# One more unit of a gated recurrence read "by squares", with four small moves around it, in a fused recurrence and SwiGLU kernel

## The chip, the cores and the metric

The kernel runs on one core of a Trainium2 chip. The metric is the device time of one execution in microseconds (us). The kernel before takes 600.96 us, the median of three runs between 600.88 and 601.17 us.

## The reference, cut to what matters

There are 4 batches, 8 heads, 768 time steps and a head dimension of 48. The recurrence's output is laid out as 3072 tokens of 384 values and goes through a feed-forward block.

```python
f = 1.0 / (1.0 + np.exp(-f_logit))
for t in range(S):
    state = f[:, :, t, :, None] * state + np.einsum('bhd,bhe->bhde', k[:, :, t], v[:, :, t])
    y[:, :, t] = np.einsum('bhd,bhde->bhe', q[:, :, t], state)
x = y.transpose(0, 2, 1, 3).reshape(B * S, H * D)          # 3072 x 384
g = x @ w_gate                                             # 384 x 1536
out = (g / (1 + np.exp(-g)) * (x @ w_val)) @ w_out         # 1536 x 384
```

The weights arrive as 64-bit floats and the four recurrence inputs as 32-bit floats.

## The kernel before, in words

**Tiling.** A *unit* u is one batch b of one chunk c of 128 time steps; there are 6 chunks of 4 batches, so u = 4c + b runs from 0 to 23. Within a unit the recurrence is done in closed form: running products of f scale k and q, TensorE forms the 128 x 128 scores (`sc`), VectorE masks them (`A`), and TensorE adds the part from the state (`y`) and forms the chunk's contribution to the next state (`dS`). A chunk's outputs of all four batches form `xT[c]`, 384 features by 512 tokens, on which the feed-forward block of that chunk runs while the next chunk's units are computed. This case concerns chunk 0's end and chunk 1 (units 4 to 7), which lie in the first 140 us. Chunk 0's feed-forward (`mlp_plain`) consists of 12 *gate* products and 12 *val* products (L808; I number them 0 to 11, in the order gate 0, val 0, gate 1, val 1, gates 2 and 3, vals 2 and 3, and so on in pairs), and then 12 *down* steps (L831) of four matrix products each, one per batch. The outputs of gate, val and down steps take turns in four PSUM banks (tag `m`): each may start when the bank's older tile has been read, a gate by ScalarE's Silu (L818), a val by VectorE's multiply (L822).

**Two ways to turn f, k and q.** They arrive with time on the partitions and are needed with features on the partitions. Units 0 to 5 use TensorE transposes (L595, four per input). From unit 6 on, `by_squares(u)` holds: four DMAs per input (L447) lay the data out so that VectorE's 32 x 32 stream transposes finish the job (f in L609, k in L620, q in L658). Units 6 and 7 also send their decayed k through DRAM instead of transposing it on TensorE (L676): VectorE turns it in squares (L642), four DMAs write it (L645) and one reads it back as `kt` (L683), all on GpSimd's queue.

**Weights.** A piece of 64-bit weights is fetched by SyncE's queue (L472, four buffers `w64`), read by two ScalarE passes (`sizes`: L489 into `up`, L491 into `top`, two buffers each) and put together by four VectorE instructions (`join`: L500, L502, L504, L506). An `up` buffer is free again after its L506.

**Order.** Each engine's order up to about 45 us is written by hand, and from there it follows the program: `attention_steps(1)` cuts each unit of chunk 1 into four steps, which `take_turns` interleaves with the gate, val and down pieces. The loads of v, and of f, k, q for units before 6, are issued by SyncE's queue (L455); v of units 6 and 7 and the loads by squares of those units are issued by GpSimd's. `load(B + 1)` loads unit 5. The least product of each unit is kept in `least`; for units by squares ScalarE copies it (L652).

Of the kernel before, what the change touches and what calls it, by code (L numbers as in the profile page):

```python
# [290 lines left out]
def short_path(ctx, tc, ident, least, judge, q, k, v, f_logit, moe_w_gate, moe_w_val, moe_w_out, out):  # L291
# [9 lines left out]
    nc = tc.nc  # L301
    B, H, S, D = q.shape
# [13 lines left out]
    SQUARES = 2  # L316
# [47 lines left out]
    def pairs(t, off=0):  # L364
        return t[:, off:off + HP * N1].rearrange("p (a t) -> p a t", t=N1)
# [33 lines left out]
    rooms = {nm: t.rearrange("p n h w -> p (n h w)")[:, 0:Q + HP * RUN] for nm, t in both_raw.items()}  # L399

    def by_squares(u):
        return u >= SQUARES * B - 2

    def make_rooms(pool):
        for nm in "fkq":
# [3 lines left out]
    def v_of(u):  # L409
        return vs[u % (NV if units[u][1] < SQUARES else NV // 2)]  # L410
# [20 lines left out]
    def load(u, what="fkqv"):  # L431
        b, c = units[u]
        rows = slice(c * C, (c + 1) * C)
        inputs = dict(f=f_logit, k=k, q=q, v=v)
        for nm in "fqkv" if c >= SQUARES else "fvkq" if by_squares(u) else "fkqv":
            src = inputs[nm]
            if nm not in what:
                continue
            if nm == "v":
                dst = v_of(u)  # L440
            elif not by_squares(u):
                dst = raw[nm][u % NRAW]
            else:
                since = len(traced)
                for n in range(4):
                    at = Q * (1 - n % 2)
                    (nc.sync if c >= SQUARES else nc.gpsimd).dma_start(  # L447
                        out=rooms[nm][Q * n:Q * (n + 1), at:at + HP * RUN].rearrange("t (a e) -> t a e", a=HP),
                        in_=src[b, n // 2::2, rows, :].rearrange("a (t i) d -> t a (i d)", i=NI))
                if c < SQUARES:  # L450
                    by_pool.extend(ins for ins in traced[since:] if ins.engine == mybir.EngineType.Pool)
                    keep_order(by_pool[-5:])
                continue
            queue = nc.gpsimd if c < SQUARES and by_squares(u) else nc.sync
            queue.dma_start(out=dst[:, :, 0:D], in_=src[b, :, rows, :].rearrange("h t d -> t h d"))  # L455

    def weight_piece(dst, src, parts):
# [60 lines left out]
    fetches, sizes, joins = [], [], []  # L518
# [29 lines left out]
    def bank(name):  # L548
        return banks[-1].tile([128, 512], FP32, tag="a", name=name)
# [10 lines left out]
    def attention(u):  # L560
        b, c = units[u]
# [30 lines left out]
        def transposed(name, src):  # L592
            p = bank(name)
            for a in range(HP):
                nc.tensor.transpose(p[:, a * C:(a + 1) * C],  # L595
                                    src[:, 2 * a:2 * a + 2, :].rearrange("t r d -> t (r d)"), ident)
            return p.rearrange("p (a t) -> p a t", t=C)
# [6 lines left out]
        else:  # L604
            p = transposed("fTp", fr)
# [22 lines left out]
        whole = pairs(tail)[:, :, 1:2]  # L628
        nc.vector.reciprocal(pairs(start)[:, :, 0:1], whole)
        yield  # L630
        if not in_squares:
            kp = transposed("kTp", kr)
            qp = transposed("qTp", qr)
            if by_squares(u + 1):
                load(u + 1)
# [13 lines left out]

        if in_squares:  # L650

            nc.scalar.copy(least[:, u, :], whole.rearrange("p a t -> p (a t)"))  # L652
            whole = least[:, u, :].unsqueeze(2)
        nc.vector.tensor_tensor_scan(gate[:, 0:n], gate[:, 0:n], start, 1.0, op0=ALU.mult, op1=ALU.add)
        yield
# [17 lines left out]
        if c < NCH - 1 and not turned:  # L673
            p = bank("kt")
# [21 lines left out]
        if c and b < B - 1:  # L696
# [20 lines left out]
            for h in range(H):  # L717
                a, par = h // 2, h % 2
# [31 lines left out]
        if c < NCH - 1:  # L750
            p = bank("dS")
# [4 lines left out]
        if c >= SQUARES and u + 2 < len(units):  # L756
            load(u + 2, "v")
# [7 lines left out]
    def load_after(u, what):  # L765

        if u + 1 < len(units) and u + 1 != SQUARES * B:
            load(u + 1, what)

    def attention_steps(c):  # L770

        runs = [attention(c * B + b) for b in range(B)]
        order = sorted((2 * b + s, b, n) for b in range(B)
                       for s, n in enumerate((1, 8, 3, 3) if by_squares(c * B + b) else (3, 6, 3, 3)))
        return [lambda b=b, n=n: [next(runs[b]) for _ in range(n)] for _, b, n in order]
# [9 lines left out]
    def keep_order(mine):  # L785
        for a, b in zip(mine, mine[1:]):
            tc.add_manual_dep(b, a.name, mybir.DependencyInfo(mybir.DependencyClass.NoSync,
                                                              mybir.DependencyReason.DATA), reason="order")
# [89 lines left out]
    whole = NJ * TRIPLE + 7 * DOWN  # L878
# [328 lines left out]
    def weights():  # L1207
        if fetches:
            fetches.pop(0)()
        if sizes:  # L1210
            sizes.pop(0)()
        if joins:
            joins.pop(0)()
# [5 lines left out]
    mark = traced[-1]  # L1219
    keep_warm(5)  # L1220
    first = [attention(b) for b in range(B)]
    done = [0] * B

    def run(b, *steps):
        for s in steps:
            assert done[b] == s
            done[b] += 1
            for _ in range((3, 1, 5, 3, 3)[s]):
                next(first[b])
# [27 lines left out]
    sizes.pop(0)()  # L1257
    run(B - 1, 3)
    first_join(("add",))
    sizes.pop(0)()  # L1260
    joins.pop(0)()
    run(B - 1, 4)

    hidden, last = mlp_plain(0)
    steps = attention_steps(1)
# [7 lines left out]
    joins.pop(0)()  # L1273
    hidden[1]()
    weights()
    load(B + 1)
    hidden[2]()
    steps.pop(0)()
    in_order(mark, (mybir.EngineType.PE, mybir.EngineType.DVE, mybir.EngineType.Activation, mybir.EngineType.SP))
# [29 lines left out]
    for c in range(2, NCH):  # L1309
        for b in range(B):  # L1310
            run = attention(c * B + b)
            waiting += [((c - 2) * whole + t, lambda run=run: next(run)) for t in times(c)[b]]
# [33 lines left out]
def kernel(  # L1346
# [22 lines left out]
    def judge(bank):  # L1369
# [13 lines left out]
        yield  # L1383

    short_path(tc, ident, least, judge, *args)
    with tc.If(redo[0] > 0, label="redo"):
        general_path(tc, *args)
# [32 lines left out]
```

## Time and profile before

| what | value |
|---|---|
| median of three runs | 600.96 us |
| the profiled execution | 601.18 us |
| its span on the core | 599.4 us |
| granted TensorE clock | 0.999 |
| busy share of the span: TensorE, VectorE, ScalarE, GpSimd | 98%, 80%, 49%, 15% |
| HBM read and written | 46.27 and 7.34 MB |

The profiled execution has 1.78 us outside its span and lies 0.22 us above the median. A row of the timeline gives a start, a duration, the engine, the line of the kernel, the operation, out<-in, and in brackets the idle time just before it with what ended it. Rows of the same form that follow each other are merged, with their count; the duration is then that of the whole row. Successive instructions overlap by some 0.07 us, so that the distance between two starts is what an instruction costs its engine.

### The profile page before, as it was taken

The numbers are of one execution on the slowest core, as the hardware profiler recorded it, in microseconds if no ns is written. First come the engines' busy times: TensorE is split into PE (matmuls) and PEld (weight loads), VectorE is DVE, ScalarE is ACT, GpSimd is POOL, SyncE is SP. The second block draws the span as 40 slices with busy tenths as digits, with TensorE's granted clock in tenths as the row PEclk, the third lists the DMA queues.
The fourth block names the chain that finished last, engine by engine and source line by source line (L and its number), as shares of the span: only waits on it lengthen the run. The fifth ranks groups of instructions, "written<-read, shape, count | busy, mean of one in ns | idle before, by whom it ended". The sixth has DMA issues, their size and how long they took to land.

```text
span 599.4 us, 10862 instructions
## 1 busy us (share of the span) xinstructions
PE 588.4 (98%) x3996; PEld 485.5 (81%) x3996; DVE 481.9 (80%) x833; ACT 293.6 (49%) x557; POOL 92.7 (15%) x211
## 2 busy tenths in 40 slices
PE   7899999999999999999999999999999999999996
PEld 5744545667888899888899888899988899988896
DVE  7999998978999977998995978995878972666741
ACT  2577854115776422576740576632376730356600
POOL 1101135100030240121130030320030320000000
PEclk9999999999999999999999999999999999999999
DMA  9999664124332144442444422343230100100001
GB/s 196 259 276 312 189 191 116 25 71 138 81 77 56 46 114 113 128 101 67 102 114 105 131 72 70 95 112 99 81 104 26 28 9 6 54 1 2 1 1 55
DMA packets 104058, 57.33 MB, mean 96 GB/s; under 512 B 65632, under 2 KB 95712, under 8 KB 104000
## 3 DMA queue, kind: packets, MB, share of 16 engines
q1 hardware_dynamic: 95552, 46.09, 29.4%
q0 software_dynamic: 6432, 7.75, 4.5%
q10 hardware_dynamic: 2016, 2.75, 1.3%
q8 instruction: 32, 0.52, 0.4%
q14 instruction: 26, 0.21, 0.1%
HBM read 46.27 MB, written 7.34 MB: 89 GB/s over the span
## 4 chain that ended last, share of the span: by engine, by line
PE 97%; DVE 2%; ACT 0%; issue 0%; DVEq 0%; ACTq 0%
PE o L1109 20%; PE A L1010 18%; PE B L1010 14%; PE c L1010 6%; PE o L1010 6%; PE o L831 5%; PE gate L808 5%; PE val L808 5%; PE sc L672 4%; PE o L1172 3%; PE y L712 3%; PE y L733 2%; PE dS L753 2%; PE y L708 1%; PE kt L676 1%; PE fTp L595 0%
## 5 line engine op out<-in xcount | busy, mean ns | idle before, releaser
L723 POOL DMA_DIRECT2D xT<-yT x120 | 60.0, 508 | 50.4 <-ACT yT L716 45.2
L1010 PE MATMUL A<-xs,w_both 128*128 128x256 f32 x240 | 62.2, 382 | 0.0
L1109 PE MATMUL o<-w_out,h 128*128 128x192 f32 x360 | 62.0, 327 | 0.0
L1109 PEld LDWEIGHTS o<-w_out,h 128*128 128x128 f32 x360 | 58.7, 190 | 1.2 <-DVE h L962 0.3
L1015 ACT COPY c<-A 128x512 f32<-128x512 f32 x40 | 23.3, 583 | 60.8 <-PE A L1010 60.7
L1015 ACT COPY aside<-A 128x512 f32<-128x512 f32 x60 | 35.2, 586 | 34.0 <-PE A L1010 33.9
L911 DVE TENSOR_TENSOR c<-c,aside 128x512 f32<-128x512 f32 x60 | 41.2, 686 | 12.5 <-ACT aside L1015 11.1
L1010 PEld LDWEIGHTS A<-xs,w_both 128*128 128x128 f32 x240 | 44.9, 190 | 6.6
L962 DVE TENSOR_TENSOR h<-h,c 128x256 f32<-128x256 f32 x100 | 40.6, 414 | 7.6 <-ACT h L1026 7.3
L687 DVE TENSOR_TENSOR A<-sc,causal 128x512 f32<-128x512 f32 x48 | 31.0, 687 | 15.7 <-PE sc L672 15.7
L914 DVE TENSOR_TENSOR c<-c,aside 128x512 f32<-128x512 f32 x60 | 41.0, 684 | 2.5 <-ACT aside L1015 2.5
L1026 ACT ACTIVATE h<-c 128x256 f32<-128x256 f32 x100 | 39.2, 416 | 6.6 <-DVE c L911 5.1
L1109 PE MATMUL o<-ws,h 128*128 128x192 f32 x240 | 41.5, 328 | 0.2 <-DVE A L687 0.2
L1010 PE MATMUL A<-xs,extra 128*128 128x256 f32 x160 | 41.2, 380 | 0.0
L1010 PE MATMUL B<-xs,w_both 128*128 128x256 f32 x160 | 41.2, 380 | 0.0
L1010 PE MATMUL c<-xT,w_both 128*128 128x256 f32 x160 | 41.1, 379 | 0.0
L1010 PE MATMUL B<-xT,extra 128*128 128x256 f32 x160 | 41.0, 379 | 0.0
L662 POOL MEMSET gates<- 128x4 f32 x24 | 2.6, 110 | 244.7 <-DVE qT L575 238.9
L1109 PEld LDWEIGHTS o<-ws,h 128*128 128x128 f32 x240 | 39.1, 190 | 0.8 <-DVE A L687 0.4
L1015 ACT COPY aside<-B 128x512 f32<-128x512 f32 x60 | 35.1, 585 | 8.3 <-PE B L1010 7.1
L911 DVE TENSOR_TENSOR c<-c,o 128x384 f32<-128x384 f32 x15 | 8.3, 552 | 36.1 <-PE o L1109 36.1
L914 DVE TENSOR_TENSOR c<-o,c 128x512 f32<-128x512 f32 x40 | 27.4, 686 | 11.9 <-ACT h L1026 6.2
(154 smaller groups left out, 1223.7 us busy)
## 6 DMA issues: line engine op xcount, KB each, us to landing
fsquares<-in_f_logit_dram SPq DMA_DIRECT2D x64, 96.0 KB, 2.5
qsquares<-in_q_dram SPq DMA_DIRECT2D x64, 96.0 KB, 2.2
ksquares<-in_k_dram SPq DMA_DIRECT2D x64, 96.0 KB, 2.3
w<-in_moe_w_gate_dram SPq DMA_DIRECT2D x6, 768.0 KB, 6.0
w<-in_moe_w_val_dram SPq DMA_DIRECT2D x6, 768.0 KB, 6.0
w<-in_moe_w_out_dram SPq DMA_DIRECT2D x6, 768.0 KB, 6.7
v<-in_v_dram SPq DMA_DIRECT2D x22, 192.0 KB, 2.8
out_dram<-ob ACTq DMA_DIRECT2D x14, 192.0 KB, 2.0
```

The source lines that it names most:

```text
L672: nc.tensor.matmul(sc[par][:, a * C:(a + 1) * C], lhsT=kT[r, a, :], rhs=qT[r, a, :], start=True, stop=True)
L687: nc.vector.tensor_tensor(A[:, par], sc[par].rearrange("p (a t) -> p a t", t=C), causal.unsqueeze(1).broadcast_to((128, HP, C)), ALU.mult)
L723: (nc.gpsimd if c >= SQUARES else nc.sync).dma_start(out=xT[c][f % 128:f % 128 + n, f // 128, b * C:(b + 1) * C], in_=yT[r:r + n, par, a / ...
L808: nc.tensor.matmul(p, lhsT=w[:, j, i, :], rhs=xT[c][:, i, :], start=(i == 0), stop=(i == KT - 1))
L831: nc.tensor.matmul(p, lhsT=hidden_tile(h, n // 2)[:, n % 2 * 2 + b // 2, b % 2 * C:(b % 2 + 1) * C], rhs=w_out[:, j, :], start=(n == 0), s ...
L911: nc.vector.tensor_tensor(dst, a, b, ALU.add)
L914: nc.vector.tensor_tensor(dst, a, b, ALU.subtract)
L962: lagging.append(lambda: f(*args))
L1010: nc.tensor.matmul(p[name][:, n, :], lhsT=weights_of[a][:, n, j, :], rhs=tokens[b], start=fresh and n == 0, stop=True, skip_group_check=True)
L1015: nc.scalar.copy(t, p[name])
L1026: nc.scalar.activation(dst, src[:, 0, :], AF.Silu)
L1109: nc.tensor.matmul(p[:, n, :], lhsT=lhsTs[j][:, n * C:(n + 1) * C], rhs=rhs[:, j, :], start=first and j == order[0] and n == 0, stop=j == ...
```

## The change: what it does

Unit 5 joins the units by squares. With that, its TensorE transposes of f, k, q and of the decayed k are gone, its twelve loads are issued by GpSimd's queue when unit 4's k and q have been read, and its decayed k goes through DRAM. The small copy of the least product of units 5, 6 and 7 goes from ScalarE to VectorE. v of units 1 to 5 is loaded by GpSimd's queue instead of SyncE's. At the end of chunk 0, the last unit's y (with its copy L748 on ScalarE) is put ahead of the two `sizes` passes of one weight piece. `load(B + 1)` is taken out.

```diff
     def by_squares(u):
-        return u >= SQUARES * B - 2
+        return u >= SQUARES * B - 3
...
-            queue = nc.gpsimd if c < SQUARES and by_squares(u) else nc.sync
+            queue = nc.gpsimd if nm == "v" and 0 < u < SQUARES * B else nc.sync
             queue.dma_start(out=dst[:, :, 0:D], in_=src[b, :, rows, :].rearrange("h t d -> t h d"))
...
         if in_squares:
 
-            nc.scalar.copy(least[:, u, :], whole.rearrange("p a t -> p (a t)"))
+            (nc.scalar.copy if c >= SQUARES else nc.vector.tensor_copy)(least[:, u, :], whole.rearrange("p a t -> p (a t)"))
...
     first_join(("add",))
+    joins.pop(0)()
+    next(first[B - 1])
     sizes.pop(0)()
-    joins.pop(0)()
-    run(B - 1, 4)
+    next(first[B - 1])
+    next(first[B - 1])
...
     hidden[1]()
     weights()
-    load(B + 1)
     hidden[2]()
```

In the order of the changed program, VectorE's list from its start up to the multiply of val 10 holds the same instructions as before, and seven more: one each of L609, L620, L642 and L658 (unit 5), and three copies L652. On ScalarE, the Silu of gate 9 comes after the sigmoid of unit 7 with its two table loads; before it came ahead of them.

## Prediction

> **What bounds the kernel now.** I read the busy shares first, then TensorE's waits, then busy time by stretch, then the timelines of TensorE and VectorE where the change lies. The page's first part:
>
> ```profile
> PE 588.4 (98%) x3996; PEld 485.5 (81%) x3996; DVE 481.9 (80%) x833; ACT 293.6 (49%) x557; POOL 92.7 (15%) x211
> ```
>
> TensorE is idle for 11 us of 599.4. Its waits between 28 and 140 us are one line:
>
> ```profile
> PE gate L808 <- ACT xT L748: 0.7, 1, 0.7
> ```
>
> So from 30 us on TensorE never waits, and whatever it no longer does is worth its full time as long as the others keep up. How near are they? Busy time by stretch (TensorE, weight loads, VectorE, ScalarE, GpSimd, clock, DMA share, GB/s):
>
> ```profile
> 45.00:60.00 15.00, 15.00 (x55) 7.37 (x54) 15.00 (x28) 11.37 (x15) 2.32 (x5) 1.00 0.90 312
> 60.00:75.00 15.00, 15.00 (x85) 7.89 (x84) 14.97 (x26) 12.49 (x17) 2.40 (x5) 1.00 0.63 189
> 75.00:90.00 15.00, 15.00 (x55) 6.91 (x58) 14.07 (x23) 7.72 (x10) 4.59 (x9) 1.00 0.70 190
> ```
>
> VectorE is as full as TensorE there: it converts weights at its own pace. That decides the case.
>
> **What TensorE saves.** Its timeline:
>
> ```profile
> 32.62 0.60 PE L595 MATMUL fTp<-idf,fraw 128*128 128x128 f32 x4
> 33.06 2.74 PE L808 MATMUL val<-xT,w_both 128*128 128x512 f32 x6
> ...
> 79.02 0.66 PE L676 MATMUL kt<-idf,kT 128*128 128x128 f32 x4
> 79.51 5.32 PE L808 MATMUL gate<-xT,w_both 128*128 128x512 f32 x12
> ```
>
> From start to start, four transposes cost 0.44 us, those of decayed k 0.49. Unit 5 loses f, k, q (three times 0.44) and decayed k: 1.81 us. The y copy: gate 0 waited 0.71 us, until 29.95, for the copy of y, which stood behind two passes (28.48 and 28.99, 0.65 and 0.53 us) and ran at 29.43 for 0.47. Unit 3's y ends by 28.63 (27.42 plus 1.21), so the copy now ends near 29.1, and gate 0 is held by unit 3's dS instead, which ends at 29.23: 0.7 us won. The passes move back by 0.5 us; the join that needs the second started at 30.06, and slips by about 0.1. Together TensorE comes 2.5 us earlier to everything after 79 us. Alone this would give 601.18 - 2.5 = 598.7, or 598.5 as a median (the profiled execution is 0.22 above it).
>
> **What VectorE has to do more.**
>
> ```profile
> 69.55 1.13 DVE L609 STREAM_TRANSPOSE gates<-fraw 128x512 f32<-128x512 f32 x1
> 70.50 0.61 DVE L504 TENSOR_SCALAR up<-w 128x768 uint16<-128x768 uint16 x1
> ...
> 86.77 0.70 DVE L620 STREAM_TRANSPOSE qT<-kraw 128x512 f32<-128x512 f32 x1
> 87.40 0.91 DVE L506 CUSTOM_DVE_ANT_0 w_out<-top,up 128x1536 uint16<-128x1536 uint16 x1
> ...
> 89.34 0.68 DVE L642 STREAM_TRANSPOSE kraw<-kT 128x512 f32<-128x512 f32 x1
> 89.96 0.66 DVE L658 STREAM_TRANSPOSE tails<-qraw 128x512 f32<-128x512 f32 x1
> ```
>
> By starts: f 0.95, k 0.63, decayed k 0.62, q 0.59 (the next instruction starts at 90.55): 2.79 us. The copies of `least` are 128x4 like the reciprocal L629, which costs 0.10 (98.74 to 98.84): three make 0.3. The multiplies by the gates cost 0.68 from PSUM or SBUF, so nothing is saved: 3.1 us more. In the changed order all seven stand ahead of the multiply of val 10, with the same work as before otherwise. Now the place where TensorE meets VectorE:
>
> ```profile
> 100.89 0.64 DVE L822 TENSOR_TENSOR h<-h,val 128x512 f32<-128x512 f32 x1
> ...
> 102.38 2.74 PE L831 MATMUL o<-w_out,h 128*128 128x384 f32 x8
> ...
> 102.65 0.69 DVE L822 TENSOR_TENSOR h<-h,val 128x512 f32<-128x512 f32 x1 [1.13 <-PE val L808]
> ...
> 105.06 1.16 PE L672 MATMUL sc<-qT,kT 48*128 48x128 f32 x16
> ```
>
> The first down step fills four banks, 0.67 us each (102.38 to 105.06); the third is val 10's. It starts at 103.72, and val 10's multiply ends at 101.53: 2.2 us of slack. VectorE's idle times of 1.13 here and 2.9 just after come too late to help. Afterwards the multiply ends at 101.53 + 3.1 = 104.6, and the third block starts at about 104.7 with a handover of 0.1: **1.0 us later than before, with the 2.5 us already spent in waiting** (val 11's multiply ends 0.6 later, in time for the fourth block). VectorE next waits for unit 6's scores, idle 2.9 us, so the shift of 1.0 stays.
>
> **The other moves.** GpSimd gets 12 loads of unit 5 (0.55 each: 2.21 for four at 57.01), a turn of 2.92 and a read-back of 0.73: 10.3 us, and five v at about 1.03 (two took 1.15 and 0.90). It is busy 18 us of 75 between 30 and 105. Unit 6's k now queues behind unit 5's turn, near 66 instead of 72.6; VectorE wants it near 79: no cost. On ScalarE unit 5's sigmoid waits for its f, loadable from 33.2 (unit 4's f read), so landed near 40 (2.2 of issue, 4.9 to landing). Behind it queue weight passes and gate 2's Silu; ScalarE idled 2.15 and 1.16 us around 42.5, which holds a table load of 1.28 and the 0.63: no cost. Were f 3 us late, gate 2's bank would still be free for gate 4, at 53.65 before.
>
> While GpSimd issued unit 6's turn (90.32 to 93.24), L502 took 0.76, L500 0.72, L504 0.76, against 0.55, 0.55, 0.61 elsewhere: 0.5 us lost. While it issued unit 6's loads (57.01 to 59.22), two L500 took 1.13 and two L502 1.08: nothing lost. Unit 5's turn therefore costs 0 to 0.5 us; I take 0.25, as fewer such instructions stand beside it. [...]
>
> SyncE loses five v and unit 5's f, k, q. Its w_val fetch at 37.77 stood behind those since 33.3; it comes 4.5 us earlier, worth at most VectorE's one wait for a fetch, 0.43 us; I take 0. GpSimd can issue v of units 1, 2, 3 from 3.3 us, not 9.58, 16.27, 18.36. Between 4 and 12 us the DMAs moved 1.71 MB, so one v takes 0.9 us, three 2.7. Unit 1's f landed at 6.64 and was used at 6.69; TensorE waits 1.15 us before unit 0's scores at 10.05, which covers that much. The cost is 0 to 1.6; I take 0.1, since later loads had over 2 us in hand (unit 2's f: landed 10.4, used 12.54) and lose the v ahead of them.
>
> **Sum.** 1.0 + 0.25 + 0.1 = 1.35: 601.18 + 1.35 = 602.5 in the profile, 602.3 as a median, slower. By the extremes of these terms, and with the 0.43 of the fetch gained: 601.5 to 604.1.
>
> **Rivals.** *Cover (faster):* VectorE runs ahead, on earlier weights and fewer waits for ScalarE, so that val 10's multiply is at most 0.9 us late instead of 3.1; from there it is faster by 1.2 or more, fully hidden 598.5. For it: VectorE's waits of 0.9 on `top` and 0.43 on a fetch. Against: 15.00 and 14.97 us busy of 15.
> *ScalarE's order:* VectorE is covered, but gate 9's Silu now stands behind unit 7's sigmoid. The L506 that frees the `up` buffer started at 85.91; in the changed order it has 3.6 us more and 2.8 less ahead of it: free near 87.7. Then 0.94 + 0.82 (passes) + 1.29 + 0.54 + 1.29 + 0.59: the Silu ends at 93.2. Gate 11 takes that bank, half way from 91.98 to 97.23 before, so at 94.6, and at 92.1 now: 1.2 us of waiting, 599.7. [...] In this trace the load at 91.47 is followed by its sigmoid at 92.76: 1.29, with no drain. In the forecast this wait is part of the longer one.
> *Start:* the three early v hold unit 1's f for all of 2.7 us: 602.3 + 1.5 = 603.8. For it: f used 0.05 us after landing. Against: the SyncE queue's loads are issued first.
>
> **Chances.** Less than 0.2% (1.2 us) cannot be told from no change. Forecast 0.60 (601.5 to 603.4; a quarter of it within the bound), start 0.11, ScalarE's order 0.13 (half of it within), cover 0.10, gain and waits cancelling 0.06. That makes slower 0.56, same 0.28, faster 0.16. The range 599.8 to 603.9 leaves out the cover, half of ScalarE's case and a little above.
>
> **What would show it.** Right: TensorE waits on VectorE at L831 near 102 to 105 (2 to 3 us) and on ScalarE at gate 11, while gate 0 starts near 29.2; VectorE without idle to 105; unit 6's scores near 106. Wrong: L831 without a wait, scores near 103 (cover); gate 0 later than 29.9 (start).

## The result and the profile after

| what | before | changed |
|---|---|---|
| median of ten runs on one chip | 601.04 us (600.71 to 601.25) | 602.12 us (601.74 to 604.01) |
| ratio, 95% interval | | 1.0022 [1.0014, 1.0030] |
| span of the profiled execution | 599.4 us | 600.0 us |

Slower by 1.1 us: the forecast was 602.3. The prediction counted less than 1.2 us as not to be told from no change; the interval of the ten runs still leaves no change out. The profiled execution took 601.75 us, among the fastest of the ten. The changed kernel's busy shares, TensorE and VectorE first:

```profile
PE 587.3 (98%) x3980; PEld 483.4 (81%) x3980; DVE 484.4 (81%) x840; ACT 292.2 (49%) x553; POOL 107.7 (18%) x233
```

TensorE has 16 matmuls less and is busy for 1.1 us less, and the kernel is slower. TensorE's waits between 28 and 145 us (engine, line and tile, releaser: total, times, longest) have new entries in place of the wait for the copy of y:

```profile
PE o L831 <- DVE h L822: 1.7, 1, 1.7
PE gate L808 <- ACT h L818: 0.8, 1, 0.8
```

Busy time by stretch, in the columns used before:

```profile
60.00:75.00 15.00, 15.00 (x79) 7.38 (x78) 14.73 (x28) 8.01 (x10) 8.86 (x14) 1.00 0.59 174
75.00:90.00 15.00, 15.00 (x92) 7.78 (x91) 14.11 (x24) 7.05 (x9) 3.36 (x7) 1.00 0.93 283
90.00:105.00 15.00, 12.42 (x30) 5.18 (x29) 14.89 (x26) 8.30 (x12) 7.73 (x14) 1.00 0.43 108
```

In the last stretch VectorE is full (14.89 of 15) and TensorE idles for 2.6 us: the engine that sets the pace has changed there. TensorE's timeline:

```profile
29.35 2.84 PE L808 MATMUL gate<-xT,w_both 128*128 128x512 f32 x6
...
77.11 5.42 PE L808 MATMUL gate<-xT,w_both 128*128 128x512 f32 x12
...
93.35 2.84 PE L808 MATMUL gate<-xT,w_both 128*128 128x512 f32 x6 [0.83 <-ACT h L818]
...
101.18 1.45 PE L831 MATMUL o<-w_out,h 128*128 128x384 f32 x4
104.38 1.56 PE L831 MATMUL o<-w_out,h 128*128 128x384 f32 x4 [1.74 <-DVE h L822]
105.87 1.16 PE L672 MATMUL sc<-qT,kT 48*128 48x128 f32 x16
```

Against the profile before, gate 0 is 0.60 us earlier (29.95), gate 8 is 2.40 earlier (79.51), and unit 6's scores are 0.81 later (105.06). Everything that was won up to 77 us is lost at two places. The two multiplies that hold the second one, on VectorE:

```profile
103.68 1.25 DVE L822 TENSOR_TENSOR h<-h,val 128x512 f32<-128x512 f32 x2
107.06 1.29 DVE L687 TENSOR_TENSOR A<-sc,causal 128x512 f32<-128x512 f32 x2 [2.14 <-PE sc L672]
```

Val 10's stood at 100.89 before. VectorE is idle only after it, for 2.14 us, while TensorE works off the late down step. The 0.81 us stays: the first product of chunk 1's MLP (L1010) starts at 141.48 instead of 140.67.

### The profile page after: what moved, and what is told of

Read it like the earlier page. It is cut to its first block, busy times and chain, and to the rows that moved or that the text cites. A ratio compares the mean times of both kernels' runs of the same rounds, so it can differ in the third digit from the quotient of the medians.

```text
span 600.0 us, 10856 instructions
## 1 busy us (share of the span) xinstructions
PE 587.3 (98%) x3980; PEld 483.4 (81%) x3980; DVE 484.4 (81%) x840; ACT 292.2 (49%) x553; POOL 107.7 (18%) x233
## 4 chain that ended last, share of the span: by engine, by line
PE 82%; DVE 4%; issue 1%; ACT 1%; DVEq 0%
PE o L1109 20%; PE A L1010 18%; PE B L1010 14%; PE o L1010 6%; PE c L1010 6%; PE o L831 5%; PE sc L672 3%; PE o L1172 3%; PE y L712 2%; PE y L733 1%; PE y L708 1%; PE dS L753 1%; DVE top L500 0%; DVE h L822 0%; DVE extra L914 0%
## 5 line engine op out<-in xcount | busy, mean ns | idle before, releaser
L1010 PE MATMUL A<-xs,w_both 128*128 128x256 f32 x240 | 62.2, 382 | 0.0
L1010 PEld LDWEIGHTS A<-xs,w_both 128*128 128x128 f32 x240 | 44.9, 190 | 6.6
L1010 PE MATMUL A<-xs,extra 128*128 128x256 f32 x160 | 41.2, 380 | 0.0
L1010 PE MATMUL B<-xs,w_both 128*128 128x256 f32 x160 | 41.2, 380 | 0.0
L1010 PE MATMUL c<-xT,w_both 128*128 128x256 f32 x160 | 41.1, 379 | 0.0
L1010 PE MATMUL B<-xT,extra 128*128 128x256 f32 x160 | 41.1, 379 | 0.0
```

The source lines that it names most:

```text
L1010: nc.tensor.matmul(p[name][:, n, :], lhsT=weights_of[a][:, n, j, :], rhs=tokens[b], start=fresh and n == 0, stop=True, skip_group_check=True)
```

## Experiments

The question was which of the two waits sets the end, and what each part of the change is worth. Where an expectation says "orders held", the changed kernel's schedule on TensorE, VectorE and ScalarE is written out as lists of its instruction numbers, so that one move moves nothing else. No run holds the orders without a move; in four of the seven held runs gate 8 starts between 77.10 and 77.12 us (77.11 in the changed kernel), in the others at 76.95, 77.37 and 77.71. A wait here costs more than its bracket says: gate 10 takes 3.67 us to gate 11's start where six such matmuls take 2.62 elsewhere, so the wait of 0.83 costs 1.05.

**Unit 7's chain behind the multiplies.** The held order of VectorE, around the move:

```diff
-(1084, 1085), (1099, 1100), (1108, 1109), (1098, 1098), (922, 922), (959, 959), (1003, 1005)
+(1084, 1085), (922, 922), (959, 959), (1099, 1100), (1108, 1109), (1098, 1098), (1003, 1005)
```

Numbers 922 and 959 are the multiplies of val 10 and 11.

> The changed kernel with the order of TensorE, VectorE and ScalarE held as it was, but for one move: the five VectorE instructions of unit 7 (scan L626, reciprocal L629, copy L652, scan L654, k's transpose L620: 3.2 us from 100.46 to 103.68) stand behind the multiplies of val 10 and 11 instead of ahead of them. Theory (VectorE's lateness at the first down step sets the end): the wait of 1.74 us at L831 goes, val 10's multiply runs near 100.5, unit 6's scores start near 104.1 instead of 105.87, and the median falls by 1.7, from 602.1 to 600.4; the wait of 0.8 at gate 11 stays. Rival 'ScalarE's order' (the wait at gate 11 is what costs): the wait at L831 moves somewhere else and the time stays at 602.1. Rival 'start or contention' (early v, the turn): 602.1 too. Unit 7's scores (122.33) get their q later by 1.1; if that shows, 0.3 to 0.6 comes back.

Measured: 600.08 us, ratio to the kernel before 0.9987 [0.9978, 0.9995]. TensorE's timeline of this run:

```profile
93.61 2.84 PE L808 MATMUL gate<-xT,w_both 128*128 128x512 f32 x6 [0.82 <-ACT h L818]
96.28 5.31 PE L808 MATMUL val<-xT,w_both 128*128 128x512 f32 x12
101.44 2.74 PE L831 MATMUL o<-w_out,h 128*128 128x384 f32 x8
104.11 1.16 PE L672 MATMUL sc<-qT,kT 48*128 48x128 f32 x16
```

The four blocks of the first down step (a block is the part that fills one bank) run without a break, and the scores start where the theory had them (104.1). This execution lost 0.26 us early, when TensorE waited for a late fetch of unit 3's f, so that gate 8 started at 77.37; from gate 8 on the scores come 2.02 us earlier than in the changed kernel:

```profile
18.45 0.63 PE L595 MATMUL fTp<-idf,fraw 128*128 128x128 f32 x4 [0.58 <-DMA fraw<-in_f_logit_dram]
```

That is more than the 1.74 us shown as idle, because by starts the wait cost 1.86 us (the first two blocks took 3.20 instead of 1.34) and the next two blocks 0.15 more. No instruction was taken out: the order of five VectorE instructions is worth 2.0 us, and with it the change is faster than the kernel before. The wait at gate 11 is still there.

**A smaller dose: one pair of sums moved back.**

```diff
-(844, 846), (1020, 1020)
+(844, 844), (1020, 1020)
...
-(922, 922), (959, 959), (1003, 1005)
+(922, 922), (959, 959), (845, 846), (1003, 1005)
```

> The changed kernel, orders held, with a smaller dose: the pair of weight sums L914 at 96.85 (1.2 us) stands behind val 11's multiply. Theory: val 10's multiply is 1.2 earlier, the wait at L831 falls from 1.74 to about 0.5, unit 6's scores start near 104.7, and the median is 600.9 (1.2 lower). A theory in which VectorE does not set the end expects 602.1.

Measured: 601.41 us, ratio 1.0010 [1.0002, 1.0019].

```profile
103.67 1.56 PE L831 MATMUL o<-w_out,h 128*128 128x384 f32 x4 [0.69 <-DVE h L822]
```

The third block starts 0.71 us earlier than in the changed kernel (104.38), and the time is 0.7 lower. The expected 1.2 is not reached because VectorE was later ahead of the move: val 9's multiply at 93.87 instead of 93.37. Some 0.4 us of that arose beside GpSimd's issue of unit 5's turn, where this run's rows are like those of the next run (shown under "Turn" below). End and third block move together, as the theory says.

**Gate 9's Silu ahead of unit 7's sigmoid.** On ScalarE, 823 is that Silu, 1023 the sigmoid:

```diff
-(973, 973), (975, 975), (1023, 1023), (823, 823)
+(973, 973), (975, 975), (823, 823), (1023, 1023)
```

> The changed kernel, orders held, with gate 9's Silu ahead of unit 7's sigmoid on ScalarE (it stood behind it, ending 93.30). Rival 'ScalarE's order': the wait of 0.83 at gate 11 goes and the end comes 0.8 earlier, 601.3. Theory: the wait at gate 11 goes and comes back in full at L831, 1.74 + 0.83 = 2.6 us, as VectorE is no earlier; unit 6's scores stay at 105.9 and the median at 602.1. If VectorE was itself held by that Silu (val 9's multiply started at 93.37, 0.07 after the Silu's end), up to 0.2 could be gained.

Measured: 604.19 us, ratio 1.0063 [1.0049, 1.0077]. The wait at gate 11 is gone, and the time is 2.1 us worse than the changed kernel's. TensorE's timeline:

```profile
104.89 2.39 PE L831 MATMUL o<-w_out,h 128*128 128x384 f32 x4 [3.33 <-DVE h L822]
107.21 1.95 PE L672 MATMUL sc<-qT,kT 48*128 48x128 f32 x16
```

The wait did move to L831, as expected: 3.33 us, that is 1.74 and the 1.05 of gate 11, and 0.5 because VectorE's multiply is that much later in this run (104.19; 0.4 of it from beside unit 5's turn, so not from the move). But the same four matmuls then take 2.32 us to the next start instead of 1.49, and the scores 1.88 instead of 1.09. The stretches of this run show why (the third number from the right is the granted clock):

```profile
105.00:105.50 0.50, 0.50 (x2) 0.20 (x3) 0.43 (x1) 0.00 (x0) 0.00 (x0) 0.97 0.17 44
105.50:107.00 1.50, 1.50 (x3) 0.61 (x2) 0.00 (x0) 0.00 (x0) 0.00 (x0) 0.50 0.48 100
107.00:108.50 1.50, 1.50 (x13) 1.29 (x14) 0.00 (x0) 0.00 (x0) 0.00 (x0) 0.50 0.24 48
108.50:109.00 0.50, 0.50 (x8) 0.47 (x6) 0.00 (x0) 0.00 (x0) 0.00 (x0) 0.61 0.00 0
109.00:111.00 2.00, 2.00 (x10) 1.25 (x7) 1.81 (x4) 0.00 (x0) 0.00 (x0) 1.00 0.00 0
```

From about 105.5 to 108.9 TensorE has half its clock: 3.4 us, of which half is lost, 1.7 us (0.83 and 0.79 by the starts above). The mean clocks of all six executions lie low, at 0.989 to 0.996. Both theories had priced a wait at its own length and missed this. The rival is refuted all the same: the wait that it holds for the cause was taken away, and nothing was won, also without those 1.7 and 0.5 us (604.19 less 2.2 is 602.0, where the rival had 601.3).

**Both moves.** The two edits above together.

> Both moves of the two runs named chain back and silu first. Theory: with VectorE out of the way the wait at gate 11 counts, so here the same move of the Silu is worth its 0.83: unit 6's scores near 103.3, the median 602.1 - 1.74 - 0.83 = 599.6, faster than either kernel. Rival 'ScalarE's order' alone: 601.3. Rival 'start or contention': 602.1. A new wait at unit 7's scores could take up to 0.6 back.

Measured: 599.81 us, ratio 0.9980 [0.9971, 0.9989], the fastest version here.

```profile
89.69 5.42 PE L808 MATMUL gate<-xT,w_both 128*128 128x512 f32 x12
94.94 5.32 PE L808 MATMUL val<-xT,w_both 128*128 128x512 f32 x12
100.09 3.08 PE L831 MATMUL o<-w_out,h 128*128 128x384 f32 x8
103.10 1.16 PE L672 MATMUL sc<-qT,kT 48*128 48x128 f32 x16
```

No wait of TensorE between 30 and 145 us is listed any more (the first down step still takes 3.01 us instead of 2.67), and the scores start 2.77 us earlier than in the changed kernel and 1.96 earlier than before. Counted from gate 8, the same move of the Silu that cost 2.1 us above brings the scores 0.75 earlier here (26.74 us after gate 8 in the first run, 25.99 in this one). The median is 0.3 lower; the profiled execution (599.21 us) lies 0.6 below it.

**The copy of y alone**, on the kernel before:

```diff
+    joins.pop(0)()
+    next(first[B - 1])
     sizes.pop(0)()
-    joins.pop(0)()
-    run(B - 1, 4)
+    next(first[B - 1])
+    next(first[B - 1])
```

> The kernel before with one part of the change alone: the copy of y ahead of the two passes. Gate 0 starts 0.6 us earlier (29.35 instead of 29.95). By the prediction's step this is worth 0.6 to 0.7 to everything behind: 600.4. Theory (VectorE is the pace in this stretch): unit 5's q multiply on VectorE ended at 77.67 and its scores started at 77.92, so only about 0.2 of it passes that point and a wait of about 0.4 appears there: 600.8, not to be told from no change.

Measured: 600.88 us, ratio 0.9994 [0.9986, 1.0003].

```profile
29.24 1.98 PE L808 MATMUL gate<-xT,w_both 128*128 128x512 f32 x4
...
78.06 1.16 PE L672 MATMUL sc<-qT,kT 48*128 48x128 f32 x16 [0.77 <-DVE qT L575]
```

Gate 0 is 0.71 us earlier, and unit 5's scores are not (77.92 before): VectorE's q multiply holds them. They are 0.14 later, so the wait is 0.77 where 0.4 was expected.

**Without the third unit.**

```diff
     def by_squares(u):
-        return u >= SQUARES * B - 3
+        return u >= SQUARES * B - 2
...
     weights()
+    load(B + 1)
     hidden[2]()
```

> The changed kernel without its largest part: unit 5 keeps its 16 transposes on TensorE; v on GpSimd's queue, the copies of least on VectorE (units 6 and 7 only) and the y copy stay. Theory: there is no wait at the first down step or at gate 11, TensorE's waits are those of the y copy's run (about 0.4 at unit 5's scores), and the time is 600.8, as for the y copy alone; so all of what the changed kernel loses belongs to unit 5. Rival 'start' (early v on GpSimd's queue costs): 601.2 to 602.5.

Measured: 601.20 us, ratio 0.9999 [0.9991, 1.0008]. There is no wait at L831 or at gate 11, and the one wait left between 28 and 145 us, 0.36 us, is at unit 5's scores as the theory had it; the small gain of the y copy is not visible. What the changed kernel loses comes with unit 5.

**More VectorE work ahead of val 10.** One, or two, more instructions are put ahead of 922 with the orders held. With one:

```diff
+    unused = first_pool.tile([128, 1], FP32, tag="unused", name="unused")
+    for n in range(1):
+        nc.vector.tensor_reduce(unused[:, n:n + 1], floor, axis=mybir.AxisListType.X, op=ALU.min)
+    more = [int(ins.name[2:]) for ins in traced[-1:]]
...
-(1098, 1098), (922, 922), (959, 959)
+(1098, 1098), (more[0], more[-1]), (922, 922), (959, 959)
```

> The changed kernel, orders held, with one more VectorE instruction ahead of val 10's multiply (a minimum over 516 elements into an unused number; 0.3 to 0.65 us). If the end only moves with VectorE, the wait at L831 is 1.74 plus that, 2.0 to 2.4, and the time 602.4 to 602.8. If a TensorE idle of that length already brings the lower clock seen in the run named silu first (granted clock 0.50 for some 3.4 us after a wait of 3.33), it is 1.7 more: 604.3.

> As the run named dose one, with two such instructions (0.6 to 1.3 us): the wait at L831 is 2.3 to 3.0. Linear: 602.7 to 603.4. With the clock drop after it: 604.4 to 605.1. A spread of over 1 us between runs would say that the drop comes in some executions and not in others.

Measured: with one, 603.05 us, ratio 1.0047 [1.0029, 1.0066]; with two, 607.17 us, ratio 1.0084 [1.0058, 1.0111]. In the profile with one, TensorE waits 2.36 us at L831 and keeps its clock (1.00 in each stretch from 102 to 112). In that with two it waits 2.92 us, and then these stretches follow:

```profile
106.50:107.00 0.50, 0.50 (x2) 0.00 (x0) 0.00 (x0) 0.00 (x0) 0.00 (x0) 0.74 0.00 0
107.00:109.00 2.00, 2.00 (x17) 1.74 (x16) 0.00 (x0) 0.00 (x0) 0.00 (x0) 0.50 0.00 0
...
113.00:114.00 1.00, 1.00 (x3) 0.53 (x2) 0.00 (x0) 0.00 (x0) 0.00 (x0) 0.72 0.00 0
```

Half clock from about 106.7 to 113.6 us, nearly 7 us. The executions fall apart by their mean granted clock. With one addition, those at 0.998 to 0.999 took 602.5 to 603.1 us, about what the linear theory has (602.4 to 602.8), and those at 0.994 to 0.995 took 604.7 to 606.8. With two, 603.2 at 0.998, 604.7 at 0.996, 606.5 to 608.3 below. So, by the mean clocks, the drop comes in three of seven executions with one addition and in five of six with two. How long TensorE waited is known only for the two profiled ones.

**v back on SyncE's queue.**

```diff
-            queue = nc.gpsimd if nm == "v" and 0 < u < SQUARES * B else nc.sync
+            queue = nc.gpsimd if c < SQUARES and by_squares(u) else nc.sync
```

> The changed kernel with v of units 1 to 4 back on SyncE's queue (unit 5's by GpSimd, as the units by squares had theirs). The prediction's steps: the early v on GpSimd's queue cost 0.1, and the w_val fetch, 4.5 us later again, brings back VectorE's wait of up to 0.43 for it; as VectorE sets the end at L831, that part would reach the end: 602.0 to 602.5. If the three early v held unit 1's f at the start (rival 'start'), gate 0 now starts earlier than 29.35 and the time is under 602.

Measured: 603.47 us, ratio 1.0036 [1.0024, 1.0049]. VectorE's waits between 25 and 106 us have a fetch among them that the changed kernel does not have, and TensorE's third block is later by as much as VectorE:

```profile
DVE up L504 <- DMA w<-in_moe_w_gate_dram: 0.8, 1, 0.8
```

```profile
104.91 1.56 PE L831 MATMUL o<-w_out,h 128*128 128x384 f32 x4 [1.75 <-DVE h L822]
```

The wait of 0.84 us ends at 38.35, and 66 us later the third block is 0.53 late (104.38). Gate 0 is no earlier (29.39 to 29.35): between these two executions the early v cost nothing at the start. The time rose by more than the profile shows; that part is not explained.

**`least` back on ScalarE.**

```diff
-            (nc.scalar.copy if c >= SQUARES else nc.vector.tensor_copy)(least[:, u, :], whole.rearrange("p a t -> p (a t)"))
+            nc.scalar.copy(least[:, u, :], whole.rearrange("p a t -> p (a t)"))
```

The three copies also move from VectorE's held list to ScalarE's.

> The changed kernel, orders held, with the three copies of least back on ScalarE, each behind the Silu nearest to it. They took 0.07, 0.12 and 0.12 on VectorE by the starts of their neighbours. Theory: val 10's multiply is 0.3 earlier, the wait at L831 falls from 1.74 to 1.4, the time to 601.8; not to be told from the changed kernel by the times alone, but by that wait. If a copy on ScalarE makes VectorE wait for it, less.

Measured: 602.20 us, ratio 1.0021 [1.0012, 1.0030]. Inconclusive: the profiled execution was the slowest of its eleven (603.94 us), with a late fetch of unit 3's f (TensorE waited 0.93 us for it at 18.80) and a wait of 0.86 for w_val, so its wait at L831 (2.01) cannot be set against 1.74. The times can't tell 0.3 us.

## Why the prediction was right, step by step

- **The mechanism.** TensorE waits at L831 for VectorE, as forecast, and the run with unit 7's chain moved back shows that this wait, and not ScalarE's order or the start, sets the end.
- **TensorE's savings.** Forecast 0.7 + 1.81; measured 0.60 at gate 0 and 2.40 at gate 8, so 1.80 for the transposes. The premise "worth its full time" held only with VectorE out of the way: the y copy alone won nothing that can be told.
- **VectorE's lateness.** Forecast 3.1, measured 2.79 at val 10's multiply (103.68 less 100.89). The seven instructions cost what was said, 3.08 us by starts. The rest is a balance of three terms that the prediction put at nothing or did not have. VectorE's waits between 25 and 106 us, before, and then in the changed kernel (the wait for val L808 comes after val 10's multiply):

```profile
DVE h L822 <- PE val L808: 1.1, 1, 1.1
DVE top L500 <- ACT top L491: 0.9, 2, 0.7
DVE up L504 <- DMA w<-in_moe_w_gate_dram: 0.4, 1, 0.4
```

```profile
DVE top L500 <- ACT top L491: 1.5, 4, 0.8
```

The wait for a fetch is gone, which wins 0.4; the waits for ScalarE's passes grew by 0.6; and the weight instructions L500 to L506 together took 0.4 less by starts. The run with v back on SyncE's queue puts the worth of that move at 0.53, by one execution of each. The prediction tied the wait of 0.43 to the w_val fetch issued at 37.77, but that wait ended at 37.15, so it was for another: the w_gate fetch issued at 31.57.
- **The third block.** Forecast 104.7, measured 104.38; the wait 1.74 instead of 2 to 3. It then costs 0.15 more, since the two blocks take 1.49 instead of 1.34.
- **Turn and start.** In the profiled execution the turn cost VectorE nothing, but it does not do so in each. GpSimd's issue of the turn, with L504 and L500 beside it, in the changed kernel and then in the run with gate 9's Silu first:

```profile
63.70 3.84 POOL L645 DMA_DIRECT2D turn<-kraw  x4 [4.43 <-DVE kraw L642]
64.97 0.59 DVE L504 TENSOR_SCALAR up<-w 128x768 uint16<-128x768 uint16 x1
65.46 0.53 DVE L500 TENSOR_SCALAR top<-top 128x768 f32<-128x768 f32 x1
```

```profile
63.69 2.96 POOL L645 DMA_DIRECT2D turn<-kraw  x4 [4.41 <-DVE kraw L642]
64.94 0.83 DVE L504 TENSOR_SCALAR up<-w 128x768 uint16<-128x768 uint16 x1
65.67 0.71 DVE L500 TENSOR_SCALAR top<-top 128x768 f32<-128x768 f32 x1
```

Either GpSimd takes 0.9 us longer or VectorE loses 0.4 us; five of the nine profiles with this turn are like the first and four like the second (L504 and L500 took 0.61 and 0.56 in the run with v back on SyncE's queue, 0.82 and 0.72 in that of `least` on ScalarE). The 0.25 taken for it thus lies between the two cases and inside its bounds, but in the profiled execution it was nothing. Why the two take longer beside each other, no run here shows. Unit 0's scores start at 10.04 (10.05 before), so the 0.1 for the early v was nothing in this execution. In two others with the early v, that of unit 7's chain moved back and that of `least` on ScalarE, unit 3's f landed late and held unit 2's scores by 0.3 and 0.6 us; none of the three profiles with v on SyncE's queue shows this, which is too few to blame the early v.
- **ScalarE's order.** Forecast: Silu of gate 9 ends at 93.2, a wait of 1.2. Measured: it ends at 93.30, and the wait is 0.83 (1.05 by starts). On ScalarE:

```profile
91.41 1.28 ACT L818 ACT_TABLE_LOAD   x1
92.70 0.60 ACT L818 ACTIVATE h<-gate 128x512 f32<-128x512 f32 x1
```

The load and its Silu are 1.29 apart, as the load and its sigmoid were before (91.47 and 92.76), so the table load costs what it cost before. It starts 0.02 us after the end of unit 7's sigmoid (90.76 plus 0.63), so nothing stands between the two. The forecast's "part of the longer one" is what the Silu run showed: taken alone, its removal only feeds the wait at L831.
- **Sum.** Forecast 1.35, of which 0.35 for the turn and the start; on TensorE's timeline 0.81; by the medians 1.08. The profiled execution itself was forecast at 602.5 and took 601.75, 0.57 above the one before: TensorE's last matmuls still come 0.81 later (L1172 at 591.22 instead of 590.41), and 0.2 of that is won back after them. So the mechanism was right and the 1.0 was near (0.81), but that the median came within 0.2 us of the forecast is in part luck: what other executions took beyond the profiled one stands where the 0.35 was put. Two of the ten, at mean clocks of 0.996 and 0.995, took 603.7 and 604.0 us; after what the added work showed, a clock drop in them is likely, but no trace here shows it. A third took 603.1 at a full clock, which is not explained.

## What to carry to other kernels

Work taken from the busiest engine is worth only as much as the next engine's slack at the point where the two meet: here the slack was 2.2 us, the next engine came 2.8 us later, and 2.4 us of savings were lost. Before giving up such a change, look at what stands ahead of the meeting point and need not: five instructions that nothing wanted yet were worth 2.0 us. And test a wait by removing it together with the one behind it, since a wait that feeds a later one is worth nothing, or less, alone.

## What was not expected of the hardware

TensorE's clock fell to half (0.50) in mid-kernel, after waits of 3.33 and 2.92 us, and not during them. In the runs with gate 9's Silu first and with two additions, the mean clocks of the stretches put the fall at 105.47 and 106.74, 0.6 and 1.2 us after the matmuls had begun again (104.89 and 105.54), and the half clock lasted 3.4 and 6.8 us. From the start of the third block to that of unit 6's y (L708) these two traces took 12.14 and 13.78 us, against 10.52 in the run with one addition: the drop cost 1.6 and 3.3 us over and above the wait.

The wait of 2.36 us in the run with one addition was followed by no such drop, nor were those of 0.69 to 2.01 us at L831 in four other traces, where the two blocks after the wait took 1.49 us and the scores 1.09, as at full clock. No trace has a wait there between 2.36 and 2.92 us. The mean clocks of the executions make it likely that the drop comes in some executions of one kernel and not in others, but only one trace of each kernel is there, and no run shows what decides it. Why the drop lasted twice as long after the shorter of the two waits is open.
